# One stationary block of 128 columns per head: values and decay weights side by side in a fused attention and MLP kernel

## The chip, the cores and the metric

The kernel runs on one core of a Trainium2 chip. The metric is device time in microseconds (us), the median of several executions. A profiled execution also has a span, from its first to its last instruction, which is about 1.8 us shorter than its time. The engines are PE (TensorE, the matmuls), PEld (its weight loads), DVE (VectorE), ACT (ScalarE), POOL (GpSimd) and SP (SyncE, here an issuer of DMAs).

A run is called slow when it lies over 1.5% above the fastest run of the same kernel. Every ratio below is the mean time of one kernel's fast runs over the mean time of the other's fast runs of the same rounds on the same chip, so it is not quite the ratio of the medians beside it.

## The reference

Attention with a decay, 8 batches of 8 heads, 576 positions of width 64, and an MLP with gelu over the resulting 4,608 tokens (512 to 2,048 to 512):

```python
s_pos = np.maximum(s, 0.0)
cum = np.cumsum(s_pos, axis=-1)
bias = -(cum[:, :, :, None] - cum[:, :, None, :])
scores = np.where(causal, -1e9, q @ k.T / 8 + np.minimum(bias, 0.0))
attn = softmax(scores)            # + 1e-9 in the denominator
x = (attn @ v)                    # heads side by side: (4608, 512)
out = gelu(x @ w_in) @ w_out      # exact gelu
```

A decay of this kind factors: exp(-(cum_i - cum_j)) is a weight of the key j times a factor of the query i, and the query's factor cancels in the division. So the kernel multiplies the values by a weight w_j, and needs for each head the sum of P_ij w_j v_j and the sum of P_ij w_j.

## The kernel before

A head's value sum and its denominator are separate matmuls with 64 output columns each; the two heads of a pair sit on columns 0 to 63 and 64 to 127 of the array. The denominator's stationary operand is the weight column, broadcast to 64 columns, so the denominator arrives already copied to all 64 partitions of its head. `MAIN` holds the four products that make positions 0 to 511, `REST` the two of the last 64.

```python
def av_mm(b, p, out, parts, den):
    for n_part, (jt, lo, n, off) in enumerate(parts):
        for e in range(2):                                    # the two heads of pair p
            h = 2 * p + e
            nc.tensor.matmul(
                out[e * 64 : e * 64 + 64, lo : lo + n],
                lhsT=(wb[:, jt, b * H + h : b * H + h + 1].to_broadcast([128, 64])
                      if den else vv[b % 2][:, jt, h, :]),
                rhs=P_of[b, p][:, e, off : off + n], ...)

def norm(b, p0, p1, num, den, i0, i1, chunks):
    ln = work.tile([128, CUT], fp32, tag="ln", bufs=2, name="ln")
    for c, lo, hi in chunks:                                  # two halves of 256
        nc.scalar.activation(ln[:, lo:hi], den[:, lo:hi], func=AF.Ln, scale=math.exp(-LNC[c]))
    nc.scalar.activation(ln[:, :w], ln[:, :w], func=AF.Exp, scale=-1.0)
    for c, lo, hi in chunks:
        # ... cut of the ring buffer xT left out
        nc.vector.scalar_tensor_tensor(out, cut(num), math.exp(-LNC[c]), cut(ln), op0=MULT, op1=MULT)

def av_item(b, p, wide=False, rest=True, last=False):
    # ... (wide: one two-bank tile of the scores' slots; last: the MLP's bank)
    num, den = [ps.tile([128, 512], fp32, tag="av", bufs=3, name=n) for n in ("avn", "avd")]
    av_mm(b, p, num, MAIN, False)
    av_mm(b, p, den, MAIN, True)
    if rest:
        av_rest(b, p)
    norm(b, p, p + 1, num, den, 0, CUT, [(0, 0, 256), (1, 256, CUT)])
```

The PSUM banks are all in use: two slots of two banks for scores and first-layer sums (`sc`), three banks for the attention sums (`av`, one of them held by `avr`, the rests of a batch), one for second-layer sums (`mlp`). Tokens go through the MLP in chunks of 512. Chunk c's first layer (`h_ps`, with gelu on ACT) stands alone; its second layer (`o_ps`) is interleaved with the attention of batch c+1, so that PE always has something to do. The middle of the loop:

```python
elif nb < B:                       # nb = c + 1, c from 1
    exp_set()
    l2_item(c, 0, 0, 4)
    # ... chunk 1 does the rest of batch 1 here
    sc_item(nb, 0)                 # scores of pair 0, Exp on ACT, mask on DVE
    l2_item(c, 0, 4)
    for p in range(1, NP):
        # ... loads and transposes of the batch after
        sc_item(nb, p)
        av_item(nb, p - 1)
        l2_item(c, p, 0, 12)       # 12 of 16 second-layer matmuls
        if p == NP - 1:
            av_item(nb, p)
            norm_rest(nb)
            gelu_set()
        l2_item(c, p, 12)
```

And the end of chunk 0, which starts the loads of batch 3 (`pace` holds the GpSimd queue until the transposes of batch 2 have landed):

```python
    # ... transposes of batch 2 issued on SP
    nc.gpsimd.tensor_copy(pace, qkT[0][:, 1, 3, 0:1])
    load_qk(3)
    load_v(3)
    absmax_v(1)
```

## Time and profile before

The kernel took 331.57 us, the median of 3 runs (331.54 to 332.82). The first fence is from the page of the profiled execution: the span, part 1 (busy time, share of the span, instructions) and part 4 (the chain of waits, followed back from the last instruction).

```profile
span 329.9 us, 6402 instructions
PE 320.2 (97%) x2585; PEld 164.0 (50%) x2585; DVE 193.1 (59%) x384; ACT 202.8 (61%) x288; POOL 65.7 (20%) x100
...
PE 86%; DMA 9%; POOL 3%; issue 0%; DVE 0%; POOLq 0%
```

PE is busy throughout, and in the chain DVE has 0% and ACT does not appear. The waits of PE between 60 and 270 us, the six chunks in the middle, are an empty list in this kernel. So PE's own work sets the time there.

The second fence is the timeline of PE around pairs 2 and 3 of batch 4 (start in us, duration in us, engine, line, operation, output<-inputs, shapes, count; square brackets would show an idle time before the group and what ended it). Ends of matmuls are modelled and overlap, so read the starts.

```profile
157.95 0.61 PE L376 MATMUL sc_ps<-qkT 64*128 64x256 bf16 x10
158.50 0.57 PE L414 MATMUL avn<-P,vv 128*64 128x256 bf16 x8
158.90 0.55 PE L414 MATMUL avd<-P,wb 128*64 128x256 bf16 x8
159.29 0.23 PE L414 MATMUL avr<-P,vv 128*64 128x64 bf16 x4
159.35 0.23 PE L414 MATMUL avr<-P,wb 128*64 128x64 bf16 x4
159.51 2.76 PE L514 MATMUL o_ps<-w_out_r,gT 128*128 128x512 bf16 x12
162.20 0.57 PE L414 MATMUL avn<-P,vv 128*64 128x256 bf16 x8
162.61 0.55 PE L414 MATMUL avd<-P,wb 128*64 128x256 bf16 x8
```

Pair 2's attention products take from 158.50 to 159.51: 1.01 us. Eight products start within 0.40 us (six of 256 columns and two of 128; a line prints the shape of its first), which is 0.05 us each: the two heads run at the same time on their halves of the array. Pair 3 follows 12 second-layer matmuls later, 2.69 us after 159.51, without a bracket: its banks were free.

The table gives the time from the first matmul of one chunk's first layer to that of the next, read from starts in the timeline; chunk 7 includes everything to the end.

| | us |
|---|---|
| start of chunk 0 | 20.79 |
| chunk 0 | 39.17 |
| chunk 1 | 35.02 |
| chunks 2 to 6 | 34.55 to 34.56 each |
| chunk 7 to the end | 62.19 |

### The profile page before, as it was taken

The page shows a single profiled execution, that of the slowest core. Times are in us where ns is not written, and L with a number is a line of the kernel's source. Part 1 is how long each engine was busy: PE and PEld are TensorE (multiplying, and loading weights), DVE is VectorE, ACT ScalarE, POOL GpSimd, SP SyncE. Part 2 cuts the span into 40 slices and gives each one's busy share as a digit, 9 for nine tenths or more (in the row PEclk, how much of TensorE's full clock was granted, in tenths as well). Part 3 has the DMA queues.
Part 4 walks back from the last instruction along what each step waited for, and adds up shares of the span by engine and source line. Part 5 has one row for each costly group of instructions (what it writes and reads, how often), then busy time and mean ns, then how long its engine had stood idle before and what let it go on. Part 6 is the DMA issues. An engine that isn't in the chain of part 4 may idle for free.

```text
span 329.9 us, 6402 instructions
## 1 busy us (share of the span) xinstructions
PE 320.2 (97%) x2585; PEld 164.0 (50%) x2585; DVE 193.1 (59%) x384; ACT 202.8 (61%) x288; POOL 65.7 (20%) x100
## 2 busy tenths in 40 slices
PE   8999999999999999999999999999999999999992
PEld 3564555445544555445544554455445544444452
DVE  5757568895669265946494748655783663150021
ACT  3897747759566857677577757677759666205400
POOL 8744243006200820710053003100000000000000
PEclk9999999999999999999999999999999999999998
DMA  7999999855975899999679655527500100010012
GB/s 113 220 209 204 207 198 254 280 91 92 251 249 115 148 260 265 178 161 228 206 147 237 178 162 131 134 105 170 137 5 34 65 35 2 32 64 32 3 64 72
DMA packets 53828, 47.30 MB, mean 143 GB/s; under 512 B 31328, under 2 KB 43872, under 8 KB 53792
## 3 DMA queue, kind: packets, MB, share of 16 engines
q0 software_dynamic: 15936, 23.07, 39.0%
q1 hardware_dynamic: 37856, 23.75, 26.8%
q8 instruction: 22, 0.36, 0.5%
q14 instruction: 14, 0.11, 0.1%
HBM read 36.85 MB, written 16.52 MB: 162 GB/s over the span
## 4 chain that ended last, share of the span: by engine, by line
PE 86%; DMA 9%; POOL 3%; issue 0%; DVE 0%; POOLq 0%
PE o_ps L514 37%; PE h_ps L495 34%; DMA w_out_r<-in_moe_w_out_dram 5%; PE sc_ps L376 5%; PE avn L414 4%; DMA w_in_r<-in_moe_w_in_dram 4%; PE avd L414 3%; PE avr L414 1%; PE o_ps L533 1%; POOL raw_v L202 1%; POOL early_k L115 1%; POOL early_q L115 1%; PE avw L414 1%; POOL w_in_r L247 0%; PE tr_ps L359 0%
## 5 line engine op out<-in xcount | busy, mean ns | idle before, releaser
L514 PE MATMUL o_ps<-w_out_r,gT 128*128 128x512 bf16 x560 | 129.4, 380 | 0.7 <-DMA w_out_r<-in_moe_w_out_dram 0.7
L495 PE MATMUL h_ps<-xT,w_in_r 128*128 128x512 bf16 x576 | 126.0, 379 | 0.6 <-DVE xT L447 0.6
L495 PEld LDWEIGHTS <-w_in_r 128*128 128x128 bf16 x576 | 56.2, 98 | 68.6 <-issue 1.0
L501 ACT ACTIVATE gT<-h_ps 128x1024 bf16<-128x1024 f32 x54 | 54.3, 1022 | 49.4 <-PE h_ps L495 49.4
L392 ACT ACTIVATE P<-sc_ps 128x1024 bf16<-128x1024 f32 x64 | 62.0, 1021 | 33.8 <-PE sc_ps L376 32.9
L514 PEld LDWEIGHTS <-gT 128*128 128x128 bf16 x560 | 51.4, 98 | 59.9 <-issue 1.0
L521 DVE COPY o_sb<-o_ps 128x512 f32<-128x512 f32 x35 | 24.0, 687 | 46.8 <-PE o_ps L514 46.7
L401 DVE TENSOR_TENSOR P<-P,tri_bf 128x512 bf16<-128x512 bf16 x58 | 23.9, 421 | 37.1 <-ACT P L392 37.0
L213 DVE TENSOR_REDUCE amx<-qkT 128x2 f32<-128x1152 bf16 x32 | 40.9, 1335 | 0.0
L447 DVE SCALAR_TENSOR_TENSOR xT<-avn,ln 128x256 bf16<-128x256 f32 (+3 forms) x64 | 21.7, 385 | 25.0 <-ACT ln L432 24.9
L202 POOL DMA_DIRECT2D raw_v<-in_v_dram x40 | 34.2, 881 | 9.6 <-DMA w_out_r<-in_moe_w_out_dram 4.2
L431 ACT ACTIVATE ln<-avd 128x256 f32<-128x256 f32 x56 | 18.6, 391 | 12.4 <-PE avd L414 11.0
L230 DVE TENSOR_TENSOR vv<-raw_v,wb 128x512 bf16<-128x512 f32 (+3 forms) x44 | 25.2, 632 | 0.7 <-DMA raw_v<-in_v_dram 0.7
L432 ACT ACTIVATE ln<-ln 128x512 f32<-128x512 f32 (+1 forms) x40 | 23.5, 587 | 1.3
L220 DVE TENSOR_REDUCE amv<-raw_v 128x1 f32<-128x2048 f32 (+1 forms) x16 | 23.0, 1471 | 1.7 <-DMA raw_v<-in_v_dram 1.7
L504 ACT ACTIVATE gT<-h_ps 128x512 bf16<-128x512 f32 x36 | 19.6, 603 | 6.3 <-PE h_ps L495 6.3
L376 PE MATMUL sc_ps<-qkT 64*128 64x256 bf16 (+2 forms) x320 | 21.4, 254 | 0.7 <-ACT P L392 0.7
L376 PEld LDWEIGHTS <-qkT 64*128 64x128 bf16 x320 | 13.3, 95 | 15.1 <-issue 12.0
L414 PEld LDWEIGHTS <-vv 128*64 128x64 bf16 x384 | 16.9, 109 | 6.8 <-issue 4.0
L414 PEld LDWEIGHTS <-wb 128*64 128x64 bf16 x384 | 17.1, 111 | 0.0
L414 PE MATMUL avn<-P,vv 128*64 128x256 bf16 x224 | 16.1, 265 | 0.0
L414 PE MATMUL avd<-P,wb 128*64 128x256 bf16 x224 | 15.4, 259 | 0.0
(94 smaller groups left out, 159.2 us busy)
## 6 DMA issues: line engine op xcount, KB each, us to landing
out_dram<-o_sb SPq DMA_DIRECT2D x35, 256.0 KB, 2.3
raw_v<-in_v_dram POOLq DMA_DIRECT2D x32, 256.0 KB, 8.7
rows<-qk_bf SPq DMA_DIRECT2D x12, 576.0 KB, 6.0
early_q<-in_q_dram POOLq DMA_DIRECT2D x14, 288.0 KB, 10.4
early_k<-in_k_dram POOLq DMA_DIRECT2D x14, 288.0 KB, 11.1
w_in_r<-in_moe_w_in_dram POOLq DMA_DIRECT2D x4, 512.0 KB, 11.5
w_out_r<-in_moe_w_out_dram POOLq DMA_DIRECT2D x4, 512.0 KB, 15.4
raw_v<-in_v_dram POOLq DMA_DIRECT2D x8, 128.0 KB, 9.9
```

Source lines behind the costliest of these rows:

```text
L202: nc.gpsimd.dma_start(out=t[:n_st, st, :, :], in_=bass.AP(tensor=v.tensor, offset=v.offset + b * H * S * D + st * 128 * D, ap=[[D, n_st], ...
L213: nc.vector.tensor_reduce(amx[:, b * NP + p], qkT[b % 2][:, :, p, :S], axis=AX, op=ALU.max, apply_absolute_value=True)
L230: eng.tensor_tensor(vb[:n_st, st0:st1, h0:h1, :], t[:n_st, st0:st1, h0:h1, :], wb[:n_st, st0:st1, b * H + h0 : b * H + h1] .unsqueeze(3).t ...
L376: nc.tensor.matmul(s_ps[:, e, off : off + n], lhsT=qkT[b % 2][e * 64 : e * 64 + 64, 1, p, jt * 128 : jt * 128 + 128], rhs=qkT[b % 2][e * 6 ...
L392: nc.scalar.activation(P[:, :, UO[u] : UO[u] + UW[u]], s_ps[:, :, : UW[u]], func=AF.Exp, scale=scale)
L401: eng.tensor_tensor(d, d, tri_bf.unsqueeze(1).unsqueeze(1).to_broadcast([128, 2, 2, 128]), op=MULT)
L414: nc.tensor.matmul(out[e * 64 : e * 64 + 64, lo : lo + n], lhsT=(wb[:, jt, b * H + h : b * H + h + 1].to_broadcast([128, 64]) if den else ...
L432: nc.scalar.activation(ln[:, :w], ln[:, :w], func=AF.Exp, scale=-1.0)
L495: nc.tensor.matmul(h_of[c, f2][i], lhsT=w_in_r[:, ko, ft * 128 : (ft + 1) * 128], rhs=xT[:, ko, c * NB % XW : c * NB % XW + NB], start=(ko ...
L501: nc.scalar.activation(gT_of[c][:, f2 * 2 : f2 * 2 + 2, :], hh_of[c, f2], func=AF.Gelu)
L514: nc.tensor.matmul(o_ps, lhsT=gT[:, ft, sub * 128 : (sub + 1) * 128], rhs=w_out_r[:, ft, :], start=(ft == 0), stop=(ft == FT - 1),)
L521: nc.vector.tensor_copy(o_sb, o_ps)
```

## The change

The intent: one 128-column stationary block per head, laid out as v0 w0 for head 0 and w1 v1 for head 1, so that one matmul gives a head's sum on 64 partitions and its denominator on the other 64. This halves the number of attention matmuls, and all of them have the full array's tiling, like the second layer's. Batch 0 keeps the old form. The price is that sum and denominator of a head lie on different partitions of one bank, so the normalisation works on 64 partitions at a time. The rest of the diff makes room: GpSimd fills the weight columns, the raw values get two buffers in place of three, the loads of batch 3 change order, some second-layer halves of chunk 0 change places, and four warm-up matmuls get narrower.

```diff
-    vv = [const.tile([128, ST, H, D], bf16, name=f"vv{i}") for i in range(2)]
+    vv = [const.tile([128, ST, NP, 4 * D], bf16, name=f"vv{i}") for i in range(2)]
...
-            raws[b, "v"] = work.tile([128, ST, H, D], fp32, tag="rawv", bufs=3, name="raw_v")
+            raws[b, "v"] = work.tile([128, ST, H, D], fp32, tag="rawv", bufs=2, name="raw_v")
...
+    def fill_w(b):
+        for st in range(ST):
+            nc.gpsimd.tensor_copy(
+                vv[b % 2][:, st, :, D : 3 * D].rearrange("j p (e d) -> j p e d", d=D),
+                wb[:, st, b * H : (b + 1) * H].rearrange("j (p e) -> j p e", e=2)
+                .unsqueeze(3).to_broadcast([128, NP, 2, D]),
+            )
... in av_item, for batches 1 to 7:
+        vw_mm(b, p, (num, den), MAIN)
         if rest:
             av_rest(b, p)
-        norm(b, p, p + 1, num, den, 0, CUT, [(0, 0, 256), (1, 256, CUT)])
+        vw_norm(b, p, p + 1, (num, den), 0, CUT, [(0, 0, 256), (1, 256, CUT)])
+
+    def vw_mm(b, p, outs, parts):
+        for e in range(2):
+            for n_part, (jt, lo, n, off) in enumerate(parts):
+                nc.tensor.matmul(
+                    outs[e][:, lo : lo + n],
+                    lhsT=vv[b % 2][:, jt, p, e * 2 * D : (e + 1) * 2 * D],
+                    rhs=P_of[b, p][:, e, off : off + n], ...)
+
+    def vw_norm(b, p0, p1, outs, i0, i1, chunks):
+        ln = work.tile([128, CUT], fp32, tag="ln", bufs=2, name="ln")
+        for e in range(2):
+            for c, lo, hi in chunks:
+                nc.scalar.activation(
+                    ln[e * D : e * D + D, lo:hi], outs[e][(1 - e) * D : (1 - e) * D + D, lo:hi],
+                    func=AF.Ln, scale=math.exp(-LNC[c]))
+        for c, lo, hi in chunks:
+            nc.scalar.activation(
+                ln[:, lo:hi], ln[:, lo:hi], func=AF.Exp, scale=-1.0, bias=lnb[:, c : c + 1])
+        ... for each head e, on its own 64 partitions r:
+                    nc.vector.tensor_tensor(
+                        xT[r, p0:p1, x0 : x0 + u1 - u0], cut(outs[e]), cut(ln), op=MULT)
...
-    keep_busy(3)
+    keep_busy(3, 256)
...
         nc.gpsimd.tensor_copy(pace, gT_of[c][:, 0, 0:1])     # chunks 2 and later
+            fill_w(nb + 1)
...
             norm_rest(0)                                      # chunk 0
+            fill_w(2)
             sc_item(1, 0)
+            l2_item(c, 1, 0, 8, av=True)
+            sc_item(1, 1)
             l2_item(c, 0, 8)
-            sc_item(1, 1)
-            l2_item(c, 1, 0, 8, av=True)
...
+            absmax_v(1)
+            load_v(3)
             nc.gpsimd.tensor_copy(pace, qkT[0][:, 1, 3, 0:1])
             load_qk(3)
-            load_v(3)
-            absmax_v(1)
...
                 norm_rest(1)                                  # chunk 1
+                fill_w(3)
```

More of the change, by code (lines that the diff above doesn't have):

```diff
@@ L159 @@
         nc.vector.memset(t[64:128, ST - 1, :, :], 0.0)
+    lnb = const.tile([128, len(LNC)], fp32, name="lnb")
+    for i, x in enumerate(LNC):
+        nc.vector.memset(lnb[:, i : i + 1], -x)
     nc.vector.tensor_copy(ident, ident_bf)
@@ L229, in scale_v @@
             n_st = 128 if st1 < ST else SL
-            eng.tensor_tensor(
-                vb[:n_st, st0:st1, h0:h1, :],
-                t[:n_st, st0:st1, h0:h1, :],
-                wb[:n_st, st0:st1, b * H + h0 : b * H + h1]
-                .unsqueeze(3).to_broadcast([n_st, st1 - st0, h1 - h0, D]),
-                op=MULT,
+            if h1 - h0 == 2:
+                eng.tensor_tensor(
+                    vb[:n_st, st0:st1, h0 // 2, :].rearrange("j s (x d) -> j s x d", d=D)[:, :, 0:4:3],
+                    t[:n_st, st0:st1, h0:h1, :],
+                    wb[:n_st, st0:st1, b * H + h0 : b * H + h1]
+                    .unsqueeze(3).to_broadcast([n_st, st1 - st0, 2, D]),
+                    op=MULT,
+                )
+                continue
+            for st in range(st0, st1):
+                eng.tensor_tensor(
+                    vb[:n_st, st, h0 // 2 : h1 // 2, :].rearrange("j p (x d) -> j p x d", d=D)[:, :, 0:4:3],
+                    t[:n_st, st, h0:h1, :].rearrange("j (p e) d -> j p e d", e=2),
+                    wb[:n_st, st, b * H + h0 : b * H + h1].rearrange("j (p e) -> j p e", e=2)
+                    .unsqueeze(3).to_broadcast([n_st, (h1 - h0) // 2, 2, D]),
+                    op=MULT,
+                )
+    def fill_w(b):
[4 more added lines that the diff above has]
+                .unsqueeze(3).to_broadcast([128, NP, 2, D]),
             )
@@ L417, in av_mm @@
                         wb[:, jt, b * H + h : b * H + h + 1].to_broadcast([128, 64])
-                        if den else vv[b % 2][:, jt, h, :]
+                        if den else vv[b % 2][:, jt, p, e * 3 * D : e * 3 * D + D]
                     ),
@@ L460, in av_item, with cut @@
             num, den = [ps.tile([128, 512], fp32, tag="av", bufs=3, name=n) for n in ("avn", "avd")]
-        av_mm(b, p, num, MAIN, False)
-        av_mm(b, p, den, MAIN, True)
+        if b == 0:
+            av_mm(b, p, num, MAIN, False)
+            av_mm(b, p, den, MAIN, True)
+            norm(b, p, p + 1, num, den, 0, CUT, [(0, 0, 256), (1, 256, CUT)])
+            return
+        vw_mm(b, p, (num, den), MAIN)
         if rest:
             av_rest(b, p)
-        norm(b, p, p + 1, num, den, 0, CUT, [(0, 0, 256), (1, 256, CUT)])
+        vw_norm(b, p, p + 1, (num, den), 0, CUT, [(0, 0, 256), (1, 256, CUT)])
[5 more added lines that the diff above has]
+                    lhsT=vv[b % 2][:, jt, p, e * 2 * D : (e + 1) * 2 * D],
+                    rhs=P_of[b, p][:, e, off : off + n],
+                    start=(n_part == 0), stop=n_part == len(parts) - 1,
+                    skip_group_check=True,
+                )
+    def vw_norm(b, p0, p1, outs, i0, i1, chunks):
+        ln = work.tile([128, CUT], fp32, tag="ln", bufs=2, name="ln")
+        w = (p1 - p0) * (i1 - i0)
+        for e in range(2):
+            for c, lo, hi in chunks:
+                nc.scalar.activation(
+                    ln[e * D : e * D + D, lo:hi], outs[e][(1 - e) * D : (1 - e) * D + D, lo:hi],
+                    func=AF.Ln, scale=math.exp(-LNC[c]),
+                )
+        for c, lo, hi in chunks:
+            nc.scalar.activation(
+                ln[:, lo:hi], ln[:, lo:hi], func=AF.Exp, scale=-1.0, bias=lnb[:, c : c + 1]
+            )
+        t0 = (b * S + i0) % XW
+        n = i1 - i0
+        for u0, u1 in ((0, min(n, XW - t0)), (XW - t0, n)):
+            if u0 < u1:
+                x0 = (t0 + u0) % XW
+                for e in range(2):
+                    r = slice(e * D, e * D + D)
+                    def cut(t):
+                        return t[r, :w].rearrange("d (p i) -> d p i", p=p1 - p0)[:, :, u0:u1]
+                    nc.vector.tensor_tensor(
+                        xT[r, p0:p1, x0 : x0 + u1 - u0], cut(outs[e]), cut(ln), op=MULT
+                    )
     def av_rest(b, p):
@@ L469, in av_rest @@
             rest_of[b] = ps.tile([128, 2, NP, SL], fp32, tag="av", bufs=3, name="avr")
+        parts = [(jt, 0, n, off) for jt, n, off in REST]
+        if b > 0:
+            vw_mm(b, p, [rest_of[b][:, e, p] for e in range(2)], parts)
+            return
         for den in range(2):
-            av_mm(b, p, rest_of[b][:, den, p], [(jt, 0, n, off) for jt, n, off in REST], den)
+            av_mm(b, p, rest_of[b][:, den, p], parts, den)
     def norm_rest(b):
         t = rest_of[b].rearrange("d n p i -> d n (p i)")
-        norm(b, 0, NP, t[:, 0], t[:, 1], CUT, S, [(2, 0, NP * SL)])
+        if b > 0:
+            vw_norm(b, 0, NP, (t[:, 0], t[:, 1]), CUT, S, [(2, 0, NP * SL)])
+        else:
+            norm(b, 0, NP, t[:, 0], t[:, 1], CUT, S, [(2, 0, NP * SL)])
     gT_of = {}
@@ L557, with keep_busy @@
     warm = ps.tile([128, 512], fp32, tag="mlp", bufs=1, name="warm")
-    def keep_busy(n):
+    def keep_busy(n, w=512):
         for _ in range(n):
-            nc.tensor.matmul(warm, lhsT=busy[:, :128], rhs=busy, start=True, stop=True)
+            nc.tensor.matmul(warm[:, :w], lhsT=busy[:, :128], rhs=busy[:, :w], start=True, stop=True)
     weights_scan()
@@ L567 @@
     weights_dve()
-    keep_busy(3)
+    keep_busy(3, 256)
     sc_item(0, 0, masks=False)
     tr_item(0, 1, 0)
-    keep_busy(1)
+    keep_busy(1, 256)
     tr_item(0, 1, 1)
@@ L597 @@
         load_w(1, i)
+    fill_w(1)
     for n in "qk":
@@ L651 @@
             sc_item(1, 2)
-            l2_item(c, 2, 0, 8)
+            l2_item(c, 2, 0, 8, av=True)
             scale_pair(1, 1)
             sc_item(1, 3)
-            l2_item(c, 2, 8)
+            l2_item(c, 2, 8, av=True)
             scale_pair(1, 2)
```

## The prediction

> **What bounds it now.** TensorE. PE is busy 97% of 329.9 us (part 1 of the page); the chain of waits (part 4) is 86% PE and from 41.6 us on never leaves it. ACT (61%), DVE (59%) and POOL (20%) matter only where PE waits.
>
> **What the change does to PE.** It halves the number of value and denominator matmuls of batches 1 to 7 (16 to 8 a pair), but not their streaming. In the timeline the two heads' 64-column matmuls start 3 to 4 ns apart and the next pair follows after 106 ns for 256 columns: they already overlap. Eight 128-column products of 106 or 53 ns need the same 0.75 us. What goes is the change of tiling mode: from the last rest product to the next o_ps matmul 129 ns pass where 27 ns is streaming; entering from o_ps costs about 120 ns. The Trainium skill (TensorEngine Tiling (Array Packing), Key Properties) says a change of mode drains TensorE; the trace agrees, about 0.11 us each. Saving: three pairs x 0.12 plus 0.23 for the last, 0.6 us a batch; 3.7 us in batches 2 to 7, 0.8 us in batch 1.
>
> **What it adds.** ACT, a pair: four Ln of 64x256 for two of 128x256 (step 0.26 us), two Exp of 256 (0.42) for one of 512 (0.63). DVE: two multiplies of 64x512 (about 0.69 us, step 0.61) for two of 128x256 (0.42, step 0.34). From the start of Ln to release of the PSUM banks: now 2.1 us, the denominator's 0.7; then about 2.5 and 3.1 us. POOL: five fills a batch, 3 to 5 us (estimate from its memsets), off the path.
>
> **Where this meets the path.** Pairs 0 to 2 are 5 us apart: enough. Pair 3 follows pair 2 after 12 o_ps matmuls (2.6 us). Pair 2's Ln must wait for ACT's two Exp of the scores (2.26 us after the scores start). Today pair 3 starts in the denominator's bank, free long before. After the change both banks wait for DVE: released 4.8 and 5.4 us after the scores start, while PE is ready at 4.0. I expect PE to stop 0.8 us before pair 3's first head and 0.2 us between heads: 1.0 us in each of batches 2 to 7, 6 us in all, against 3.7 saved.
>
> **Start and batch 1.** Shorter warm-up matmuls (0.4 us) and reordered second-layer halves (the 0.68 us wait for w_out_r) bring PE forward about 1.2 us. But DVE then runs an unbroken row from the landing of raw_v (50.2 us): scaling, masks, longer multiplies, for which the first layer of chunk 1 waits. I expect nearly all of this given back there.
>
> **Sum.** 331.6 + 6 x 0.4 + 0.1 = 334; the waits may be shorter, so 333.2 us, range 330.4 to 335.8. Chances: faster by over 2% 0.02, within 2% 0.94, slower 0.04.
>
> **What would show it.** Value products of 0.75 + 0.12 us a pair without the gap before o_ps; a PE wait for DVE xT of 0.8 us before pair 3 of batches 2 to 7; ACT busy 20 us more, DVE 15 us more; no wait for w_out_r; chunk 1's first layer waiting 1 to 2 us for DVE xT.
>
> **What would make it wrong.** Ln or multiplies cheaper on 64 partitions: no stall, about 329. Fills slowing DVE's two-input scaling or delaying loads in batch 1: above 335. 128-column weight loads not hiding behind 64-column products (27 ns).

## The result and the profile after

The changed kernel is correct. It took 347.55 us, the median of 4 runs (345.37 to 350.25), against 331.56 us for the kernel before on the same chip (4 runs, 331.34 to 332.82). The ratio is 1.048, with a 95% interval from 1.039 to 1.057: slower, and above the top of the predicted range.

The page after, the same three lines:

```profile
span 347.4 us, 5840 instructions
PE 322.3 (93%) x2213; PEld 163.0 (47%) x2249; DVE 221.9 (64%) x402; ACT 234.7 (68%) x379; POOL 90.6 (26%) x135
...
PE 74%; DVE 8%; ACT 6%; DMA 5%; issue 4%; POOL 1%; SPq 0%; DVEq 0%; POOLq 0%
```

PE's busy time is nearly the same (322.3 for 320.2 us), the span is 17.5 us longer, and DVE and ACT have entered the chain. DVE is busy 28.8 us more and ACT 31.9, where 15 and 20 were predicted. The four longest waits of PE over the whole span (what waited, what it waited for, us in total, times, longest):

```profile
PE avn L495 <- DVE xT L527: 9.8, 6, 3.6
PE h_ps L566 <- DVE xT L527: 2.4, 3, 1.6
PE warm L632 <- DVE busy L125: 1.2, 1, 1.2
PE avd L495 <- DVE xT L527: 0.7, 4, 0.2
```

The third line is in the kernel before too, and there PE also waited once, 0.6 us, for `xT` at the first layer. The waits before the attention products (`avn`, `avd`) are new. By chunk:

| | before, us | after, us | difference |
|---|---|---|---|
| start of chunk 0 | 20.79 | 23.37 | +2.6 |
| chunk 0 | 39.17 | 37.91 | -1.3 |
| chunk 1 | 35.02 | 43.45 | +8.4 |
| chunks 2 to 6 | 34.55 each | 36.11 to 36.13 each | +7.8 in all |
| chunk 7 to the end | 62.19 | 62.10 | -0.1 |

So there are two losses: one chunk that is 8.4 us longer, and five that are 1.55 us longer each.

**The steady chunks.** The timeline of pairs 2 and 3 of batch 4 in the kernel after, which answers to the one shown of before, now with ACT and DVE (weight loads, DMA lines and some other lines of DVE are left out):

```profile
169.42 0.61 PE L397 MATMUL sc_ps<-qkT 64*128 64x256 bf16 x10
169.86 1.94 ACT L413 ACTIVATE P<-sc_ps 128x1024 bf16<-128x1024 f32 x2 [1.20 <-PE sc_ps L397]
169.97 0.56 PE L495 MATMUL avn<-P,vv 128*128 128x256 bf16 x4
170.36 0.55 PE L495 MATMUL avd<-P,vv 128*128 128x256 bf16 x4
170.75 0.28 PE L495 MATMUL avr<-P,vv 128*128 128x64 bf16 x4
170.88 2.75 PE L585 MATMUL o_ps<-w_out_r,gT 128*128 128x512 bf16 x12
...
171.82 0.65 ACT L508 ACTIVATE ln<-avn 64x256 f32<-64x256 f32 x2
172.50 0.64 ACT L508 ACTIVATE ln<-avd 64x256 f32<-64x256 f32 x2
173.17 0.91 ACT L513 ACTIVATE ln<-ln,lnb 128x256 f32<-128x256 f32 x2
174.10 0.68 DVE L527 TENSOR_TENSOR xT<-avn,ln 64x512 bf16<-64x512 f32 x1 [1.71 <-ACT ln L513]
174.84 0.54 PE L495 MATMUL avn<-P,vv 128*128 128x256 bf16 x4 [1.21 <-DVE xT L527]
175.57 0.56 PE L495 MATMUL avd<-P,vv 128*128 128x256 bf16 x4 [0.19 <-DVE xT L527]
```

Read the attention products first. Four matmuls (three of 256 columns, one of 128) replace eight, in 0.39 us for 0.40, and the pair's products take from 169.97 to 170.88: 0.91 us for 1.01. That tenth is the gap that used to stand before o_ps. The predicted saving is there.

Then read the chain that ends it: pair 2's scores start at 169.42, the two Exp of the scores hold ACT until 171.8, then four Ln, two Exp, the first multiply, and only then is a bank free for pair 3. PE restarts 5.42 and 6.15 us after the scores began, where 4.8 and 5.4 were predicted. It had stood still for 1.21 and 0.19 us.

The sum for this batch closes on the starts alone. Pair 3: 3.96 us from o_ps to its first product (170.88 to 174.84) for 2.69, so +1.27, and 1.24 us for its products instead of 1.02, so +0.22. Pairs 0 and 2: 0.12 and 0.10 us saved. Pair 1: 1.32 us instead of 1.01 (164.56 to 165.88), +0.31, because its second head and the next o_ps wait about 0.2 us each for DVE. That is +1.58 of the +1.55 measured.

**Chunk 1.** From the timeline of the kernel after, five groups between 69 and 98 us, in order of time:

```profile
69.52 4.20 POOL L205 DMA_DIRECT2D raw_v<-in_v_dram  x5 [12.77 <-DVE amv L223]
...
86.03 0.19 POOL L749 CAST pace<-qkT 128x1 f32<-128x1 bf16 x1 [12.31 <-DMA qkT<-rows]
86.54 0.65 POOL L101 DMA_DIRECT2D early_q<-in_q_dram  x1 [0.33 <-issue]
...
94.73 0.83 DVE L181 COPY qk_bf<-early_q 128x1152 bf16<-128x1152 bf16 x2 [4.67 <-DMA early_q<-in_q_dram]
...
97.84 0.60 PE L495 MATMUL avn<-P,vv 128*128 128x256 bf16 x4 [3.57 <-DVE xT L527]
```

The values of batch 3, moved ahead of `pace` and with one buffer fewer, first wait 12.8 us for DVE to finish with the old ones; then their transfers run at the same time as the eight transposes of batch 2, which land later. `pace` is passed at 86.0 and the loads of batch 3's queries go out at 86.5; in the kernel before they went out at 77.95. DVE stands 4.67 us at the interleaving copy, and the multiply that PE needs comes after it in DVE's row.

A stop of this length has a second price. The trace records half the clock from 98.2 to 101.6 us, directly after the stop of 3.57 us, for 3.41 us. The Trainium skill (TensorE: Matmul & The Clock Gate, "What's actually happening") says that the clock is decided in free-running windows of 3,413 ns and drops to half after an idle one. The length agrees, 3.41 us. That the window must be idle does not: in the 3.41 us just before the half clock PE worked for the last 0.35 us, and in later runs shorter stops were followed by it, of 2.88 us (late), 2.22 us (late_p1) and 1.98 us (pair3only), while one of 2.05 us in loads was not.

How long this stop is differs between executions of the same instructions. The run steps2, below, is the changed kernel up to the end of chunk 1, and there the transposes landed 1.9 us earlier:

```profile
84.17 0.19 POOL L759 CAST pace<-qkT 128x1 f32<-128x1 bf16 x1 [10.51 <-DMA qkT<-rows]
...
95.64 0.54 PE L495 MATMUL avn<-P,vv 128*128 128x256 bf16 x4 [1.42 <-DVE xT L537]
```

The stop was 1.42 us, no half clock followed, and chunk 1 took 40.59 us in place of 43.45. So 2.9 us of the 8.4 are not in every execution.

### The profile page after: what moved, and what is told of

Its sections match the earlier page's. It is cut to its first block, busy times and chain, and to the rows that moved or that the text cites. A ratio compares the mean times of both kernels' runs of the same rounds, so it can differ in the third digit from the quotient of the medians.

```text
span 347.4 us, 5840 instructions
## 1 busy us (share of the span) xinstructions
PE 322.3 (93%) x2213; PEld 163.0 (47%) x2249; DVE 221.9 (64%) x402; ACT 234.7 (68%) x379; POOL 90.6 (26%) x135
## 4 chain that ended last, share of the span: by engine, by line
PE 74%; DVE 8%; ACT 6%; DMA 5%; issue 4%; POOL 1%; SPq 0%; DVEq 0%; POOLq 0%
PE h_ps L566 34%; PE o_ps L585 27%; PE sc_ps L397 5%; DVE xT L527 4%; DMA qkT<-rows 3%; ACT P L413 2%; DMA early_q<-in_q_dram 2%; PE avn L495 2%; ACT ln L508 2%; PE avd L495 2%; PE tr_ps L380 2%; DVE o_sb L592 1%; DMA early_k<-in_k_dram 1%; PE o_ps L604 1%; ACT ln L513 1%
## 5 line engine op out<-in xcount | busy, mean ns | idle before, releaser
L585 PE MATMUL o_ps<-w_out_r,gT 128*128 128x512 bf16 x535 | 127.9, 382 | 2.3 <-issue 0.5
L585 PEld LDWEIGHTS <-gT 128*128 128x128 bf16 x560 | 52.7, 98 | 59.8 <-issue 2.1
L527 DVE TENSOR_TENSOR xT<-avn,ln 64x512 bf16<-64x512 f32 (+4 forms) x34 | 18.9, 557 | 37.2 <-ACT ln L513 37.0
L205 POOL DMA_DIRECT2D raw_v<-in_v_dram x40 | 34.5, 878 | 21.1 <-DVE amv L223 12.8
L495 PEld LDWEIGHTS <-vv 128*128 128x128 bf16 x336 | 24.7, 99 | 21.1 <-issue 9.7
L513 ACT ACTIVATE ln<-ln,lnb 128x256 f32<-128x256 f32 x63 | 28.9, 501 | 0.9
L508 ACT ACTIVATE ln<-avn 64x256 f32<-64x256 f32 x52 | 17.0, 375 | 13.1 <-PE avn L495 12.6
L253 POOL COPY vv<-wb 128x512 bf16<-128x512 bf16 x35 | 24.7, 763 | 0.0
L243 DVE TENSOR_TENSOR vv<-raw_v,wb 128x512 bf16<-128x512 f32 (+2 forms) x36 | 24.3, 736 | 0.2
L495 PE MATMUL avn<-P,vv 128*128 128x256 bf16 x104 | 14.4, 261 | 9.8 <-DVE xT L527 9.8
L527 DVE TENSOR_TENSOR xT<-avd,ln 64x512 bf16<-64x512 f32 (+4 forms) x34 | 19.4, 569 | 1.0
```

The costliest lines, as they stand in the source:

```text
L205: nc.gpsimd.dma_start(out=t[:n_st, st, :, :], in_=bass.AP(tensor=v.tensor, offset=v.offset + b * H * S * D + st * 128 * D, ap=[[D, n_st], ...
L253: nc.gpsimd.tensor_copy(vv[b % 2][:, st, :, D : 3 * D].rearrange("j p (e d) -> j p e d", d=D), wb[:, st, b * H : (b + 1) * H].rearrange("j ...
L495: nc.tensor.matmul(outs[e][:, lo : lo + n], lhsT=vv[b % 2][:, jt, p, e * 2 * D : (e + 1) * 2 * D], rhs=P_of[b, p][:, e, off : off + n], st ...
L513: nc.scalar.activation(ln[:, lo:hi], ln[:, lo:hi], func=AF.Exp, scale=-1.0, bias=lnb[:, c : c + 1])
L527: nc.vector.tensor_tensor(xT[r, p0:p1, x0 : x0 + u1 - u0], cut(outs[e]), cut(ln), op=MULT)
L585: nc.tensor.matmul(o_ps, lhsT=gT[:, ft, sub * 128 : (sub + 1) * 128], rhs=w_out_r[:, ft, :], start=(ft == 0), stop=(ft == FT - 1),)
```

## The experiments

The theory: (S) in the steady chunks the loss is the wait for PSUM banks before pair 3; (L) in chunk 1 it is the load order; (W) the later start is the narrower warm-up. The rival for all of them: the loss is the block form itself, its normalisation on DVE and ACT, wherever it runs.

### The first four: warm-up, loads, form, banks

**warm512.** The change with the four warm-up matmuls wide again.

```diff
-    keep_busy(3, 256)
+    keep_busy(3)
...
-    keep_busy(1, 256)
+    keep_busy(1)
```

> The changed kernel with its four narrow warm-up matmuls (256 columns) made 512 wide again, nothing else. Theory W (the narrower warm-up keeps TensorE from counting as busy early enough, so the full clock is granted at 19.7 us instead of 9.3 us): full clock at about 9 to 10 us, the first layer of chunk 0 starts at about 21 us instead of 23.4, and the time falls by 2 to 3 us to about 345. Rival (the moment of the clock change is luck[...]): the full clock still comes at some other moment, differing between runs, and the time stays within the changed kernel's own spread of 345.4 to 350.3.

Measured: 350.14 us (349.46 to 350.96, 4 runs), ratio 1.055 (1.050 to 1.061). Full clock was recorded from 20.2 us and the first layer began at 23.95 us, as late as without the edit. This one profile would not be enough, because the moment of the full clock differs between runs of one kernel (beforelook, below). But fillmove, with the narrow matmuls, had the full clock from 4.7 us and its first layer at 19.94. Theory W falls.

**loads.** The change with `load_v(3)` back behind `load_qk(3)`.

```diff
             absmax_v(1)
-            load_v(3)
             nc.gpsimd.tensor_copy(pace, qkT[0][:, 1, 3, 0:1])
             load_qk(3)
+            load_v(3)
```

> The changed kernel with the loads of batch 3 put back in the old order (pace, queries and keys, then values), nothing else. Theory L (the value loads, moved ahead, share the DMA engines with the eight transposes of batch 2 and make them last 20 us instead of 14; so queries and keys are issued at 86.5 us instead of 78, DVE waits 4.7 us for them, PE 3.6 us for DVE, and the clock is halved for 3.4 us): transposes land near 80 us, the query load is issued near 80, PE waits under 1 us before pair 2 of batch 2, no half clock in mid-kernel, chunk 1 takes 37 to 38 us instead of 43.5, time down 5 to 6 us to about 342. Rival (the delay of chunk 1 comes from DVE being late with the longer multiplies): chunk 1 stays at 42 us or more.

Measured: 346.25 us (344.18 to 347.12, 4 runs), 3.9 us less than warm512 of the same chip, ratio 1.041 (1.035 to 1.047). The queries' loads went out at 80.1 us, DVE no longer waited for them, and the half clock in mid-kernel was gone. Chunk 1 was 41.21 us: 2.2 less, far from the 35.02 of before. The load order is one part, but its size is not shown: steps2, with the moved loads, had 40.59, and the changed kernel's two quicker runs (345.37 and 345.92 us) lie in the range of this one. What had taken its place is in the timeline of this run, where the block fill of batch 3 now meets DVE's masks:

```profile
85.19 1.58 DVE L422 TENSOR_TENSOR P<-P,tri_bf 128x512 bf16<-128x512 bf16 x2
86.70 1.91 DVE L427 TENSOR_TENSOR P<-P,tri_bf 128x128 bf16<-128x128 bf16 x1
86.73 2.90 POOL L253 COPY vv<-wb 128x512 bf16<-128x512 bf16 x5
```

The small mask took 1.91 us; elsewhere it takes 0.22.

**oldav.** The change with everything except the block form: the old products and normalisation in all batches, and the moved loads, the fills and the narrow warm-up kept.

```diff
-        if b == 0:
+        if True:
             av_mm(b, p, num, MAIN, False)
             av_mm(b, p, den, MAIN, True)
+            if rest:
+                av_rest(b, p)
             norm(...)
...  the same in av_rest and norm_rest: if b > 0 becomes if False
```

> The changed kernel with the products and the normalisation of all batches done the old way (64-column pairs, Ln and Exp and multiplies on 128 partitions); layout, fills, buffers, load order and warm-up stay as changed. Theory R (the steady loss of 1.5 us a batch is the later release of the PSUM banks): chunks 2 to 6 take 34.5 to 34.6 us as before instead of 36.1, the PE wait before pair 3 is gone; the loss at the start and in chunk 1 stays in part; time 336 to 341. Rival (the fills, the layout or the smaller value buffer cost it): chunks 2 to 6 stay at 36 us and the time near 347.

Measured: 335.9 us (332.15 to 337.3, 4 runs, one slow), ratio 1.005 (0.997 to 1.014). Chunks 2 to 6 are 34.55 us, to a hundredth the kernel before; chunk 1 is 37.45. The block form carries the steady loss alone. In chunk 1 of this profile the moved loads and the fills cost 2.4 us without it.

**pair3bank.** The change with pair 3 of batches 2 to 7 in a two-bank slot of the scores, which is free at that time, and a first-layer pair moved in exchange.

```diff
+        sw = 2 <= c < B
...
-            l1_item(c, 1, k0, k1)
+            l1_item(c, 1, k0, k1, av=sw)
...
-        l1_item(c, 2, av=True)
+        l1_item(c, 2, av=not sw)
...
-                    av_item(nb, p)
+                    av_item(nb, p, wide=True)
```

> The changed kernel with pair 3 of batches 2 to 7 in the PSUM banks of the scores, and items 1 and 2 of the first layer of chunks 2 to 7 trading their banks so that none waits for it. Theory R (PE's stop before pair 3 is the wait for pair 2's banks): the stop of 1.2 + 0.2 us goes, chunks 2 to 6 take 34.6 to 34.9 us instead of 36.1, time down 7 to 9 us, to about 339. Rival (the stop is ACT and DVE being out of time, not banks): the wait only moves to the first layer, chunks stay above 35.7 us.

Measured: 341.0 us; two of four runs, the profiled one among them, are slow; the fast ones took 336.24 and 340.04 us, ratio 1.018 (1.009 to 1.027). The stop before pair 3 is gone, and the steady chunks are 34.53 to 34.72 us in place of 36.1. The slow profile has the long stop and the half clock in chunk 1 (43.19 us); the steady chunks lie behind that, each of them shows the gain, and no profile of the kernel with the stop comes near it, so the reading does not hang on the state. Theory S holds. But the chunks are not shorter than before's 34.55: the 0.6 us a batch that the block form saves are not in the time.

### Inside the chain, and pair 3 alone

**steps2.** A measurement. Its output is wrong, which doesn't matter for the time. In single pairs of some batches, Ln becomes a copy, with one property changed at a time: batch 3 reads both heads from one bank, batch 4 reads both from the same partitions, batch 5 takes all 128 partitions, batch 6 writes both multiplies to partitions 0 to 63, batch 7 is the unchanged pattern with the copy.

```diff
+                if one_pair and b == 3:
+                    i = outs[0][(1 - e) * D : (1 - e) * D + D, lo:hi]
+                if one_pair and b == 4:
+                    i = outs[e][D : 2 * D, lo:hi]
+                if one_pair and b == 5:
+                    o, i = slice(0, 2 * D), outs[e][:, lo:hi]
+                if one_pair and b in (3, 4, 5, 7):
+                    nc.scalar.activation(ln[o, lo:hi], i, func=AF.Copy, scale=1e-36)
...
+                    if one_pair and b == 6:
+                        r = slice(0, D)
```

> The changed kernel, wrong on purpose, to measure what makes two ACT or DVE instructions in a row not overlap. The step from the second to the third Ln (head 0 to head 1) is 0.39 us where the step within a head is 0.28. Batch 3: both heads read the same bank, other partitions. Batch 4: both read partitions 64 to 127 of two banks, but write different partitions. Batch 5: all read and write 128 partitions of two banks. Batch 7: the unchanged geometry with the same stand-in function as control. Batch 6: both multiplies of DVE on partitions 0 to 63. Theory P (a change of the partitions that an instruction works on ends the overlap): step 0.38 to 0.40 in batches 3 and 7, 0.26 to 0.29 in batch 5, and in batch 4 it tells reads from writes; DVE's step 0.61 in batch 6 instead of 0.71. Rival B (a change of PSUM bank ends it): 0.28 in batch 3, 0.39 in batches 4 and 5; DVE's step stays 0.71.

Measured, start to start of consecutive ACT instructions of 256 elements, in ns:

```
between the two halves of one head, batches 3, 4 and 7    280 to 285
batch 7, other bank and other partitions (the pattern)    391 to 393 in pairs 0 to 2
batch 4, same source partitions, other output partitions  392 to 393 in pairs 0 to 2
batch 3, one bank, other partitions                       379 to 380
batch 5, 128 partitions, other bank                       264 in pairs 0 to 2, 381 in pair 3
```

Pair 3 of batches 4 and 7 is left out: the second head's step is 459 to 460 ns there, which may be a wait for PE's products and was not tested. A change of partitions alone costs a tenth of a microsecond; a change of bank alone cost nothing in three pairs out of four, and what differed in the fourth stays open. On DVE the two multiplies of 64x512 stand 0.715 us apart, with 0.683 us of length: end to end. In batch 6, on the same partitions, they stand 0.787 us apart, but there the second overwrites what the first wrote, so this does not tell what the change of partitions does. The rule found on ACT explains 0.11 us of a chain that came out 0.6 us too long; the rest is in the section on the prediction.

**pair3only.** Built from the kernel before: the block form for pair 3 of batches 2 to 7 alone, where its two mode changes could be saved without a second block pair close by.

```diff
+        if b > 1 and p == NP - 1:
+            vw_mm(b, p, (num, den), MAIN)
+            vw_mm(b, p, [rest_of[b][:, e, p] for e in range(2)], [(jt, 0, n, off) for jt, n, off in REST])
+            vw_norm(b, p, p + 1, (num, den), 0, CUT, [(0, 0, 256), (1, 256, CUT)])
+            return
```

> The kernel before, with the side-by-side block for pair 3 of batches 2 to 7 alone (its own small weight tile, one fill a batch; everything else as before). Pair 3 stands between second-layer matmuls on both sides, and pair 2 keeps the old form, so its denominator bank is free early. Theory R (the block form saves the mode changes, and only the late release spoils it): PE does not stop before pair 3, each of chunks 2 to 6 takes 34.3 to 34.4 us instead of 34.55, time 1 to 1.5 us below before. Rival (the block form costs TensorE itself something, for instance weight loads that do not hide behind the 64-column products): chunks 34.55 us or more.

Measured: 336.87 us (335.99 to 339.11, 6 runs), ratio 1.014 (1.009 to 1.019): a miss. There is no stop before pair 3, but chunk 2 is 35.68 us and chunks 3 to 6 are 35.28 to 35.31, instead of 34.3. (Chunk 0 of this profile was 42.21 us, with a wait of 1.98 us for `w_out_r` and the half clock behind it; that is apart from the block form.) PE waits for gelu at the first layer; ACT, which must normalise pair 3's rest apart from the other rests, first waits 1.26 us for a multiply of DVE, and the table load for gelu comes behind it. I took that wait for the lack of a third buffer; p3b, below, tests it.

### Repairs, one after the other

**fillmove.** The run loads, with the fill of batch 2 moved ahead of the first layer and that of batch 3 into chunk 2.

```diff
+    fill_w(2)
     load_qk(2)
...
+            if c == 2:
+                fill_w(3)
             fill_w(nb + 1)
...  and the two fills in the attention parts of chunks 0 and 1 taken out
```

> The load order of the run 'loads', and the fills for batches 2 and 3 moved away from DVE's busy stretches (the one for batch 2 behind the value loads of batch 1, the one for batch 3 into the first layer of chunk 2). Theory F (GpSimd's copies hold up DVE's instructions with two SBUF inputs, which costs 1.6 us before the first layer of chunk 1 and 2.5 us of masks in chunk 1): the mask multiplies near 85 us take 0.4 and 0.2 us each again, chunk 1 takes 38 to 39 us instead of 41.2 in 'loads', PE's waits at the first layer of chunk 1 fall from 2.7 to about 1 us; time 2 to 4 us under 'loads'. Rival (the longer multiplies alone make DVE late): chunk 1 stays above 40.5 us.

Measured: 345.06 us (343.46 to 346.74, 4 runs), ratio 1.040 (1.033 to 1.046). Chunk 1 was 40.37 us: 0.8 less than in loads, not the 2 to 3 expected, and only 0.2 less than in steps2, which has neither repair. The collision of fills and masks in chunk 1 is the smaller part.

**allfix.** fillmove and pair3bank together.

> The changed kernel with all three repairs: load order, moved fills, banks for pair 3. If the three losses are separate and add: chunk 1 as in 'fillmove', chunks 2 to 6 at 34.6 us as in 'pair3bank', the start as it falls (full clock at 8 to 20 us); time 333 to 336, the remaining distance to the kernel before being the start and 1 to 3 us of chunk 1. If they hide each other, the sum is less than the parts and the time stays above 338.

Measured: 337.11 us (335.26 to 338.92, 4 runs), ratio 1.012 (1.006 to 1.019). Chunk 1 is 38.92 us, chunk 2 is 35.70, the later ones 34.53 to 34.72. In chunk 1 PE still waits for DVE: 2.2 us at the first layer, 0.6 before a pair.

**late.** allfix with batches 1 and 2 in the old form; the block form is left for batches 3 to 7.

```diff
-        if b == 0:
+        if b < 3:
...  the same in av_rest and norm_rest: b > 0 becomes b > 2; the fills of batches 1 and 2 go
```

> The version with all repairs, with batches 1 and 2 put back to the old products and normalisation; the block form is left for batches 3 to 7, with pair 3 in the free two-bank slot. Theory A (what is left of chunk 1's loss, 38.9 against 35.0 us, and of chunk 2's, 35.7 against 34.6, is the added VectorE and ScalarE work of batches 1 and 2, which has no slack there): chunk 1 falls to 35.0-35.4 us, chunk 2 to 34.5-34.9, later chunks stay at 34.5-34.7, and the time is 331-334 us, within 2% of before. Rival B (it is the moved loads, the reordered second layer or the bank switch): chunk 1 stays above 37 us. Rival C (the full clock comes at a different moment in each run): the start of the first layer may be anywhere between 19.9 and 24 us and moves the time by that much, whatever the kernel.

Measured: 337.46 us (333.23 to 338.28, 6 runs, one slow), ratio 1.011 (1.006 to 1.016). Chunk 1 is 35.02 us, exactly before's: theory A holds for it. (late_p1, next, has the same instructions up to the end of chunk 1 and took 36.12 there, so one profile settles this to about 1 us.) But the time did not fall, because chunk 2 became 39.17 us. Two fills, ten copies in a row, now stood there. Three groups of its timeline, one from each of POOL, DVE and PE:

```profile
112.17 5.77 POOL L253 COPY vv<-wb 128x512 bf16<-128x512 bf16 x10
...
113.31 4.91 DVE L422 TENSOR_TENSOR P<-P,tri_bf 128x512 bf16<-128x512 bf16 x2 [4.43 <-ACT P L413]
...
117.53 0.51 PE L497 MATMUL avn<-P,vv 128*128 128x256 bf16 x2 [2.88 <-DVE P L422]
```

The first of the two masks took 4.16 us by itself (0.42 otherwise). It began 0.04 us after the third copy and ended 0.35 us after the last one had started. The half clock followed the stop again, 3.41 us from 117.6.

The Trainium skill (SBUF — State Buffer, "Who interferes with whom") says that a DVE instruction with two inputs in SBUF and a GpSimd instruction that reads SBUF contend for one port, and that the loser waits until the other finishes. This trace agrees, and goes further: the copies started every 0.55 us, and the mask did not get through between them, for seven copies on end.

**late_p1.** late, with pair 1's main part in the old form in all batches.

```diff
-        if b < 3:
+        if b < 3 or p == 1:
```

> As the run before it, and pair 1 of batches 3 to 7 in the old products and normalisation too (its rest in the block form). Theory A (in the later chunks the block form takes about 0.48 us of matmul time out of a batch, and the three stops of 0.2 us give it back: before pair 1's second head, at the output block after it, at the first layer): with pair 1 in the old form its second stop goes, chunks are 34.2-34.5 us, and the time is 1 us under the other. Rival B (the stops come from the normalisation as a whole being later, not from pair 1): the stop moves to pair 2 or to the first layer, and the chunks stay at 34.5-34.7.

Measured: 336.12 us (332.15 to 337.12, 6 runs), ratio 1.009 (1.004 to 1.014). Chunk 2 is 38.40 us, again with a mask of 3.50 us beside the ten copies. Chunks 3 to 6 are 34.53 to 34.71 us, as in late. That is rival B's time, but not its mechanism: the stop did not move. Pair 1 of batch 5, now in the old form:

```profile
192.84 0.57 PE L435 MATMUL avn<-P,vv 128*64 128x256 bf16 x8
193.46 0.57 PE L435 MATMUL avd<-P,wb 128*64 128x256 bf16 x8
```

Its two banks are 0.62 us apart, for 0.41 in the kernel before. What makes it wait is the pair before it, not its own form: in late2_p0, below, where pair 0 is in the old form and pair 1 in the block form, pair 1's are 0.40 us apart.

**p3b.** pair3only with three normalisation buffers, a moved fill and the new second-layer order in chunk 0.

```diff
-        ln = work.tile([128, CUT], fp32, tag="ln", bufs=2, name="ln")
+        ln = work.tile([128, CUT], fp32, tag="ln", bufs=3, name="ln")
```

> Pair 3 alone in the block form (batches 2 to 7), built from the kernel before, with three buffers for the normalisation instead of two, the second-layer order of the changed kernel in chunk 0 and the block fills spread. Theory A (the 35.3 us of the first such version came from the ScalarE wait of 1.26 us for a normalisation buffer, which made the gelu late): that wait is gone, PE no longer waits 0.8 us for gelu, chunks are 34.2-34.6 us, and the time is 329-333 us. Rival B (the extra instructions of pair 3's rest are in the way of gelu by themselves): chunks stay above 35 us.

Measured: 337.04 us (335.8 to 338.5, 6 runs), ratio 1.014 (1.011 to 1.017), chunk 2 35.68 us and chunks 3 to 6 35.28 to 35.31 (chunk 1 was 36.31, for 34.79 in pair3only). The wait of ACT is there unchanged, 1.26 us before the Ln of pair 3's rest, so the buffer was not its reason; what else orders the two (both work on the tile of the rests) was not tested. Theory A falls, and the time stays where rival B put it. PE's waits over the whole span, first line:

```profile
PE h_ps L568 <- ACT gT L574: 5.3, 6, 1.2
```

**beforelook.** The kernel before, unchanged, one look.

> The kernel before, one look, for the moment of the full clock and the start of the first layer. If the moment is set by something other than the kernel, it lies anywhere between 4 and 21 us here, and the start of the first layer between 19.9 and 24; if the change moved it, it is 9.3 and 20.8 us again. Chunks 2 to 6: 34.55 us.

Measured: 334.06 us, one run of unknown state, span 332.3 us. The first layer began at 24.25 us, later than in any other trace here. The first full-clock record stands at 20.57 us; in the profile shown of the same kernel it stood at 9.28. The windows view from 9.4 to 20.5 us, in that profile and then in this one (window, length, PE busy and its matmuls, then the other engines, the granted clock and DMA):

```profile
9.40:20.50 11.10, 10.26 (x210) 7.61 (x208) 7.92 (x17) 9.88 (x17) 6.52 (x13) 1.00 1.16 222
```

```profile
9.40:20.50 11.10, 10.27 (x145) 6.15 (x145) 7.58 (x15) 7.09 (x10) 7.10 (x13) 1.00 1.16 220
```

210 matmuls in one and 145 in the other, in the same 11.1 us. (The view's clock, 1.00 in both, knows only what was recorded, and before the first record nothing was; the counts decide.) The later start of the kernel after, +2.6 us, and the shorter chunk 0 behind it are therefore within what the kernel before does by itself.

### Closing the account

Open at this point: no run had all the losses away at once.

**late2.** late, with the fills of batches 3 and 4 moved ahead of the first layer, where nothing uses those columns.

```diff
         load_w(1, i)
+    fill_w(3)
...
     load_v(1)
+    fill_w(4)
...
-            if c == 2:
-                fill_w(3)
-            fill_w(nb + 1)
+            if c > 2:
+                fill_w(nb + 1)
```

> The version with the block form only in batches 3 to 7, with the block fills of batches 3 and 4 moved out of chunk 2 to the two places before the first layer where the changed kernel with repairs filled those of batches 1 and 2. Theory A (the 39.2 us of chunk 2 in the run before it came from ten GpSimd copies that ran for 5.8 us without a pause beside a VectorE mask, which took 4.16 us in place of 0.42, and from the clock lost in the stop): no mask takes over 1 us in chunk 2, the stop of 2.9 us and the half clock are gone, chunk 2 is 34.6-34.9 us, and the time falls by 4 to 4.5 us to 332-334 us, the same as before within 1%. Rival B (batch 3's first block products need more than that): chunk 2 stays above 36 us.

Measured: 333.72 us (332.38 to 334.21, 6 runs) against 331.94 for the kernel before (11 runs), ratio 1.003 (0.999 to 1.007): the same. Chunks 1 to 6 are 35.03, 35.05, 34.72, 34.69, 34.54 and 34.72 us. No mask of the attention in chunk 2 took over 0.43 us, and the clock stayed full from 17.4 to 331.4 us. The account closes: with four causes taken away (the load order, the fills beside masks, the work added to batches 1 and 2, the bank wait of pair 3) the block form, in batches 3 to 7, costs within 1% what the old form costs, and gains nothing. From chunk 1 to the end the two profiles differ by 1.2 us, of which about 0.3 lie in chunk 7, where every run with the changed banks of pair 3 is longer. Pairs 1 and 2 of batch 5 in this run show why:

```profile
189.34 0.61 PE L397 MATMUL sc_ps<-qkT 64*128 64x256 bf16 x10
189.94 0.56 PE L497 MATMUL avn<-P,vv 128*128 128x256 bf16 x4
190.56 0.54 PE L497 MATMUL avd<-P,vv 128*128 128x256 bf16 x4
190.94 0.28 PE L497 MATMUL avr<-P,vv 128*128 128x64 bf16 x4
191.19 3.61 PE L587 MATMUL o_ps<-w_out_r,gT 128*128 128x512 bf16 x16
194.74 0.61 PE L397 MATMUL sc_ps<-qkT 64*128 64x256 bf16 x10
195.28 0.56 PE L497 MATMUL avn<-P,vv 128*128 128x256 bf16 x4
195.68 0.55 PE L497 MATMUL avd<-P,vv 128*128 128x256 bf16 x4
```

Pair 2's heads are 0.40 us apart (195.28 to 195.68), pair 1's 0.62: its second bank came free 0.2 us late. After pair 1 the next o_ps starts 0.25 us behind avr, where 0.12 is usual. The saving is visible in the same trace: 0.12 and 0.10 us in pairs 0 and 2, and for pair 3 0.10 us on entry (2.59 us for 12 o_ps matmuls and the change, for 2.69) and 0.14 in its products. It is given back in stops of 0.1 to 0.2 us, those of pair 1 and one at the first layer (0.7 us in all in four waits for DVE), that are too short to have been noticed in a sum of waits.

**late2_p0.** late2, with the main part of pair 0 in the old form too, so that pair 1 finds its banks free.

```diff
-        if b < 3:
+        if b < 3 or p == 0:
```

> As the run before it, with the main part of pair 0 of batches 3 to 7 in the old form as well. Theory A (the stop before pair 1's second head and the one at the output block are pair 0's longer normalisation, which holds the bank that pair 1 needs): both go, chunks 3 to 6 are 34.2-34.5 us and the time is 1 us under the other. Rival B (any pair in the block form pushes VectorE and ScalarE so that a stop shows up somewhere else): chunks stay at 34.5-34.7. Either way within 1% of the kernel before.

Measured: 334.19 us (332.8 to 335.81, 6 runs), ratio 1.005 (1.001 to 1.010). Chunks 3 to 6 are 34.66 to 34.84 us. The stop has left pair 1 and stands before pair 2's second head:

```profile
194.72 0.56 PE L497 MATMUL avn<-P,vv 128*128 128x256 bf16 x4
195.34 0.54 PE L497 MATMUL avd<-P,vv 128*128 128x256 bf16 x4
```

0.62 us between the heads of pair 2, for 0.40 in late2. Rival B. In late2, late_p1 and this run alike the stop stands at the first pair that follows a block pair, whatever its own form. The stop does not add up from pair to pair: in late2 pair 2 follows pair 1 after 5.34 us, where pair 1 followed pair 0 after 5.04, and its heads are 0.40 us apart. No version beat the kernel before.

## Why the prediction was right or wrong

The prediction said 333.2 us, from 330.4 to 335.8. Measured were 347.55. The saving and the kind of wait were right; what failed were the length of the normalisation chain and the missing cost of batch 1.

**Right: what PE saves.** "What goes is the change of tiling mode", about 0.12 us a pair and 0.6 a batch. The Trainium skill (TensorEngine Tiling (Array Packing), "Key Properties") says that a change of mode drains TensorE, and the traces agree, in that the gap before o_ps goes with the change of tiling: 1.01 to 0.89 us for a pair. In late2 the terms are 0.12 + 0.10 + 0.24 for pairs 0, 2 and 3; with about 0.12 for pair 1, hidden under its stops, that is 0.6 again. The wait of 0.68 us for w_out_r went, as predicted, and the first layer of chunk 1 waited 2.2 us for DVE (1.60 and 0.58), a little over the predicted 1 to 2. Also right was the form of the main loss, a stop before pair 3 and a shorter one between its heads, and pair3bank confirmed its cause.

**Wrong in size: the chain of the normalisation.** The step was "From the start of Ln to release of the PSUM banks: now 2.1 us, the denominator's 0.7; then about 2.5 and 3.1 us", and with it "released 4.8 and 5.4 us after the scores start". Measured, from Ln to PE's restart, 3.02 and 3.75 us, and 5.42 and 6.15 after the scores. The terms, all from the trace of batch 4:

- The first Ln waits until ACT's second Exp of the scores has ended, 2.40 us after the scores, not 2.26. In the kernel before, Ln started 0.1 us inside that Exp.
- The Ln follow at 0.284, 0.393 and 0.280 us, not at 0.26. The long one is the change of partitions (steps2).
- The Exp of 256 took 0.50 us, not the 0.42 of the old one. It now has its bias in a column of memory instead of none. The Trainium skill (ScalarE: Activation LUTs, "What ACT_TABLE_LOAD costs") gives about 93 ns for each such operand; the trace shows 0.08 us. This could have been looked up.
- The two multiplies stand 0.715 us apart, not 0.61.

The first three come to 0.4 to 0.5 of the 0.62 us by which the first bank was late (an estimate from these figures, since the two Exp overlap); the rest is not accounted for.

The stop itself was 1.4 us for the predicted 1.0. The prediction then set the saving of 0.6 against it, and had no stop in pairs 0 to 2 ("Pairs 0 to 2 are 5 us apart: enough"). Pair 1 has two, +0.31 us net, because its second head and the output copy queue behind pair 0's longer multiplies. So the chunk lost 1.55 us for the predicted 0.4; over five chunks 7.8 us for 2.0.

**Wrong: the start and batch 1.** The step was "I expect nearly all of this given back there", which entered the sum as +0.1 us. It costed the warm-up and the reordered halves, and left out the order of loads: the diff moves `load_v(3)` ahead of `pace`, and the prediction never asked what else stood behind it in the queue. Chunk 1 lost 8.4 us. In the order in which the experiments took its causes away, one profile each: load order 2.2 us (43.45 to 41.21), fills beside masks 0.8 (to 40.37), the stop before pair 3 of batch 2 1.5 (to 38.92), the longer normalisation of batches 1 and 2 on a DVE that had no slack there 3.9 (to 35.02, which is the kernel before). These shares depend on the order; oldav, which kept the loads and dropped the form, left 2.4 us. And they are single profiles: chunk 1 of the unrepaired kernel was 40.59 us in steps2, and that of late was 36.12 in late_p1, with the same instructions each time. Against the quicker kind of execution only 0.2 us is left of the 3.1 for load order and fills, and the normalisation's share lies between 2.8 and 3.9. The prediction's last paragraph named a part of it: "Fills slowing DVE's two-input scaling or delaying loads in batch 1: above 335". It was held for unlikely without being costed, and it does not name the moved value loads.

**What is left open.** The moment of the first full clock differs between runs of one kernel (9.3 and 20.6 us). Which window it falls into was not controlled, so single spans can differ by 2 us for no reason in the kernel. Why chunk 1 with the moved loads comes in two lengths (40.59 and over 43 us) was not tested. How much of the 0.3% left over in late2 is real is open too: its interval includes 1.

## What to carry to other kernels

Before halving a number of matmuls, measure whether they already overlap: here the halves ran side by side, and only the drain between tilings, 0.12 us, was to be had. A layout that is better for TensorE and splits the follow-up work by partitions gives the engines that release its banks more or longer instructions (here twice the Ln and Exp, and multiplies of 0.68 us for 0.42); cost that chain from the first input to the restart of PE, for each pair, and not only for the one that is known to be tight. And treat each line of a diff that moves a load, a fill or a buffer count as a change of its own: look at what stands behind it on the same queue, and at which two-input DVE work a GpSimd copy will run beside.

## What the Trainium skill lacked or had wrong

- ScalarE: Activation LUTs gives one figure for the overlap of consecutive activations, about 93 ns. It does not say that a change of partitions ends it: consecutive Ln of 64x256 started 0.28 us apart on the same partitions and 0.38 to 0.39 with a change of partitions, in one bank too (steps2).
- SBUF — State Buffer describes the contention for one instruction. It does not say that a row of GpSimd copies can hold a VectorE instruction off for the whole row: a mask of 0.42 us took 4.16 while copies started every 0.55 us (late).
- TensorE: Matmul & The Clock Gate says that the full clock comes around 4 us into sustained matmuls, give or take 500 ns with the window. Here it varied by 11 us between two looks at one kernel (9.28 and 20.57 us), in a start whose matmuls come in short groups. And the half clock did not need a whole idle window: stops of 2.88, 2.22 and 1.98 us were enough (late, late_p1, pair3only).
- TensorEngine Tiling (Array Packing) says that a change of mode drains, without a figure. Here it was 0.10 to 0.14 us each (1.01 to 0.89 us for a pair; 2.69 to 2.59 us on entry).
